# Fourteen commands of a one-core attention-and-MLP schedule at other places

## The chip, the core and the metric

The kernel runs on one core of a Trainium2 chip. The core has five engines, each with a queue of its own that it works through in order: TensorE (PE, matrix products; its weight loads have a row of their own in the profile, PEld), VectorE (DVE), ScalarE (ACT), GpSimd (POOL) and SyncE (SP, which here only starts transfers). They meet through semaphores. Sixteen DMA engines move data between memory and the chip; transfers are started from SP and ACT (queue q1 and q10 in the profile) and from POOL (queue q0). The metric is device time in microseconds (us), the median of several runs.

## What is computed

Attention for 4 batches of 8 heads, 768 positions, 64 values a head, and behind it an MLP whose hidden layer is the largest of three products:

```
scores = scale * q @ k.T                      # per batch and head
mask   = causal                               # heads 0, 2, 6 (retrieval)
mask   = causal & (sink | last 64 positions)  # heads 1, 3, 4, 5, 7 (near)
a      = exp(scores - max); a = a / (sum(a) + 1e-9)
x      = a @ v                                # 3072 rows of 512
h      = max(x @ w1, x @ w2, x @ w3)          # 512 -> 768
out    = h @ w_out                            # 768 -> 512
```

Inputs and output are in fp32; the products run in fp16 with fp32 sums.

## The kernel before

The order of the work is written out by hand. `PROGRAM` (lines 84 to 150) is a list of 493 short commands; the last loop of `fast` takes them one by one and calls the function that the first word names. Every engine gets its instructions in the order in which the commands issue them, so moving one command moves its instructions on every engine and every queue that it uses. Nothing is re-sorted behind that. A trailing letter names the engine of a copy (`d` DVE, `a` ACT, `p` POOL, `r` DVE in the form of a reduction over one element); `s` on a load is SP's queue.

A batch is worked in two halves of 384 positions. Batch 0 has a path of its own, so that the first scores can begin before much has landed: heads go in four pairs (0,2), (1,3), (4,6), (5,7), called hp 0 to 3. Later batches take keys and queries in two "quads" of four heads. The commands that the change and the prediction speak of:

- `hl half hp n`: loads of keys and queries of batch 0 in fp32 (SP and ACT). `cast half hp kq`: their casts to fp16, tiles `kn` and `qn`. `turnp half hp`: PE transposes them, and copies (line 241) bring them to `KQ`.
- `kx0 half hp` and `kx b quad`: copies of keys for the near heads' neighbouring blocks into `kx` (lines 561, 566; 573, 578).
- `s0 half unit hp..`: a score unit of batch 0. PE writes a mask (line 596) and the products (line 611) into one of two `st` buffers; ACT takes the exponential into `pt` (line 632). `s b n` is a score unit of the later batches (lines 677, 694). `k0` and `k` multiply a mask into `pt` (line 380).
- `load_v 0 half`: values of batch 0, three rows of a partition apart, into `vs`. `vc half h0 n`: their casts into `vn` (line 500). `vt half blocks`: PE sorts the rows by products with a 0/1 matrix `every3` (line 508) into banks `vb`, and casts bring them to `va` (line 513). `vt 0 02 da` sorts blocks 0 and 2, the first drained by DVE, the second by ACT.
- `y b half heads what`: copies values for the near heads into `vx`; `s` copies the sinks' rows (line 529), `r` the last rows (line 527).
- `av b half hp`: attention times values (line 720), normalised on DVE (lines 725, 727) into `x`. `x b half hp` transposes `x` on PE and copies it to `xT` (lines 743, 746); with `D` a DMA does that.
- `f b half w n`: a hidden unit, four products of weight w's block n with `xT` (line 440). Weight 0 is copied to `acc` (line 448), weights 1 and 2 take a maximum with it on DVE (line 452). `o`: the output product (line 465).
- `load b quad`: keys and queries of a batch's quad, cast on the way, started by POOL (line 261). `turn b quad i part`: DVE transposes them into `KQ` (line 275). `w n`: a weight's load, started by POOL. `gs n`: a tiny transfer on SP that holds SP's queue until a weight has landed. `flags`: fifteen tiny POOL operations on the flags `is_retrieval`.

Score units take the `st` buffers in turn, and products for `tr`, `vb`, `oacc` and `yy` take four banks in turn, so a unit waits until the one that held its place has been drained.

```
    for line in PROGRAM:
        for item in line.split(", "):
            name, *args = item.split()
            do[name](*args)
```

Of the kernel before, what the change touches and what calls it, by code (L numbers as in the profile page):

```python
# [83 lines left out]
PROGRAM = (  # L84
    "idle 11, hl 0 2 2 sc, cast 0 1 pd, turnp 0 1 aa, cast 0 0 dd, cast 0 2 dp, load_v 0 0 0 4 s",
    "load_v 0 0 4 4 s, turnp 0 0 ad, cast 0 3 pa, cleark 0 p, cleark 1 d, kx0 0 1 p, s0 0 1 1",
    "s0 0 0 0, hl 1 0 2 ss, idle 1, turnp 0 3 da, turnp 0 2 da, clear 0 d, s0 0 1 0, kx0 0 3 p",
    "s0 0 0 3, vc 0 0 4 p, vc 0 4 4 p, s0 0 0 1, kx0 0 2 p, s0 0 0 2, hl 1 2 2 ss, cast 1 0 dd",
    "turnp 1 0 dd, load 1 0 0, cast 1 1 pp, w 0, load 1 0 1, cast 1 3 dp, vt 0 02 da, cast 1 2 aa",
    "vt 0 1 a, turnp 1 1 d, y 0 0 1:4:2 r p, s0 0 1 2, s0 0 1 3, y 0 0 4:5:1 r r, turnp 1 3 ad",  # L90
    "s0 1 3 0, y 0 0 5:8:2 s r, kx0 1 1 p, y 0 0 1:4:2 s p, s0 1 1 1, load_v 0 1 s, turnp 1 2 dd",
    "kx0 1 2 r, y 0 0 5:8:2 r r, av 0 0 1, s0 1 2 0, kx0 1 3 p, w 1, gs 1, y 0 0 4:5:1 s p",
    "s0 1 0 1, av 0 0 0, av 0 0 3, av 0 0 2, s0 1 0 2, x 0 0 1 d, x 0 0 0 d, load 1 1, s0 1 3 2",
    "vc 1 0 4 p, x 0 0 3 a, vc 1 4 4 p, s0 1 0 0, s0 1 0 3, x 0 0 2 d, vt 1 1 a, turn 1 0 0 0",
    "clear 1 p, k0 1 1 2 p, vt 1 02 ad, turn 1 0 0 1, turn 1 0 1 1, s0 1 1 0, k0 0 0 2 p",
    "k0 0 1 2 d, f 0 0 0 3 a, k0 1 0 2 p, f 0 0 0 1 a, s0 1 1 3, w 2, y 0 1 1:4:2 r p, s0 1 1 2",
    "y 0 1 4:5:1 r r, gs 0, gs 0, gs 0, gs 0, k0 0 3 2 d, f 0 0 0 5 a, kx 1 0 a, k0 2 1 0 p",
    "turn 1 0 1 0, k0 3 0 2 p, av 0 1 0, av 0 1 1, f 0 0 0 4 a, turn 1 1 0 0, turn 1 1 0 1",
    "f 0 0 0 2 a, f 0 0 0 0 a, x 0 1 0 a, f 0 0 1 0, load 2 0, f 0 0 1 5, x 0 1 1 a, turn 1 1 1 1",
    "s0 1 2 2, k0 2 0 1 p, turn 1 1 1 0, f 0 0 1 3, f 0 0 1 2, k0 2 0 0 p, y 0 1 5:8:2 r a",  # L100
    "f 0 0 1 1, k0 3 1 2 p, f 0 0 1 4, s 1 0, av 0 1 2, kx 1 1 p, k0 2 1 1 p, k0 2 3 1 p",
    "av 0 1 3, f 0 0 2 0, f 0 0 2 1, s 1 1, x 0 1 2 a, f 0 0 2 5, k 1 0 X 1 d, k 1 1 Y 0 p",
    "f 0 0 2 2, turn 2 0 0 0, f 0 0 2 4, turn 2 0 1 0, x 0 1 3 a, s 1 2, f 0 0 2 3, f 0 1 0 5 a",
    "f 0 1 0 3 a, k 1 1 X 1 p, turn 2 0 1 1, f 0 1 0 1 d, s 1 7, k 1 2 X 0 p, f 0 1 0 2 d, flags",
    "load_v 1 0 s, v 1 0 0 d, y 1 0 1:8:2 s a, v 1 0 1 a, gs 0, k 1 2 Y 0 d, y 1 0 4:5:1 s r",
    "k 1 0 Y 0 p, f 0 1 0 0 d, w 3, v 1 0 2 d, f 0 1 1 2, s 1 3, f 0 1 2 2, f 0 1 1 1",
    "load_v 1 1 s, k 1 3 Y 0 p, f 0 1 1 3, f 0 1 2 3, y 1 0 4:5:1 r a, y 1 0 1:8:2 r a, gs 0",
    "f 0 1 0 4 d, s 1 5, k 1 0 X 0 d, k 1 1 X 0 p, load_v 2 0 s, f 0 1 1 5, f 0 1 2 5",
    "y 1 1 1:8:2 r r, k 1 7 X 1 p, y 1 1 4:5:1 r r, f 0 1 1 4, k 1 5 X 1 p, av 1 0 0 D, s 1 6",
    "load 2 1, av 1 0 1 D, v 1 1 2 d, f 0 1 1 0, v 1 0 3 a, f 0 1 2 0, f 0 1 2 1, k 1 2 X 1 p",  # L110
    "av 1 0 2 D, av 1 0 3 D, s 1 4, k 1 4 X 1 p, k 1 4 Y 0 p, f 0 1 2 4, v 1 1 3 p, o 0 0 0 a",
    "o 0 0 1 a, k 1 3 X 1 p, o 0 1 1 a, k 1 7 Y 1 d, turn 2 1 0 1, turn 2 1 1 1, k 1 4 X 0 p",
    "v 1 1 1 p, turn 2 1 0 0, turn 2 0 0 1, v 1 1 0 p, load_v 3 0 s, v 2 0 0 a, o 0 0 2 a, guess",
    "turn 2 1 1 0, f 1 0 0 1 a, f 1 0 0 0 a, f 1 0 1 0, f 1 0 0 5 d, k 1 7 X 0 p, v 2 0 1 p",
    "f 1 0 0 4 d, s 2 0, k 1 3 X 0 p, f 1 0 2 0, k 1 7 Y 0 d, load 3 0, k 1 6 X 0 p, f 1 0 1 4",
    "k 1 5 Y 0 d, v 2 0 2 a, y 2 0 1:8:2 s a, kx 2 0 d, kx 2 1 a, f 1 0 2 4, f 1 0 1 1",
    "k 1 5 X 0 d, f 1 0 0 3 a, f 1 0 1 5, f 1 0 1 3, k 1 6 Y 0 p, av 1 1 3 D, av 1 1 1 D, s 2 1",
    "k 2 1 Y 0 p, av 1 1 0 D, y 2 0 1:8:2 r a, f 1 0 2 3, k 2 0 Y 0 p, gp 1 2, f 1 0 2 1",
    "y 2 0 4:5:1 s a, av 1 1 2 D, k 2 1 X 0 p, y 2 0 4:5:1 r a, v 3 0 0 p, s 2 4, f 1 0 2 5",
    "f 1 0 0 2 d, load 3 1, y 3 0 4:5:1 r d, v 2 0 3 a, f 1 0 1 2, f 1 0 2 2, s 2 2, k 2 2 X 0 d",  # L120
    "f 1 1 0 0 d, k 2 1 X 1 p, k 2 0 X 1 p, f 1 1 0 4 a, f 1 1 1 0, y 3 0 1:8:2 s a, k 2 2 X 1 d",
    "turn 3 0 0 0, y 3 0 1:8:2 r p, f 1 1 0 5 d, load_v 3 1 s, s 2 7, f 1 1 0 2 d, k 2 0 X 0 p",
    "f 1 1 0 1 a, o 0 1 0 d, f 1 1 1 1, av 2 0 0 D, k 2 4 Y 0 d, f 1 1 1 2, f 1 1 1 5",
    "load_v 2 1 s, k 2 4 X 1 d, k 2 7 Y 1 d, f 1 1 1 4, k 2 7 X 0 d, o 1 0 2 d, s 2 3",
    "k 2 3 X 1 p, turn 3 0 1 0, gs 0, k 2 2 Y 0 d, f 1 1 0 3 a, o 0 1 2 a, av 2 0 1 D, s 2 6",
    "y 2 1 1:8:2 r a, f 1 1 2 0, k 2 6 X 0 p, av 2 0 3 D, f 1 1 1 3, k 2 7 Y 0 d, s 2 5",
    "k 2 6 Y 0 d, av 2 0 2 D, f 1 1 2 4, f 1 1 2 3, f 1 1 2 5, turn 3 1 0 1, k 2 3 X 0 p",
    "y 3 0 4:5:1 s a, o 1 0 1 a, k 2 5 X 1 p, turn 3 0 1 1, turn 3 1 1 1, k 2 3 Y 0 p, v 3 1 0 d",
    "v 2 1 2 a, o 1 0 0 a, k 2 7 X 1 p, f 1 1 2 2, f 2 0 0 0 a, f 1 1 2 1, f 2 0 1 0, k 2 4 X 0 d",
    "f 2 0 2 0, f 2 0 0 1 a, turn 3 1 1 0, f 2 0 0 2 d, f 2 0 1 2, y 2 1 4:5:1 r p, v 3 0 3 p",  # L130
    "v 3 1 2 a, v 2 1 0 a, turn 3 1 0 0, f 2 0 0 4 a, f 2 0 1 4, v 3 1 1 p, turn 3 0 0 1",
    "v 2 1 1 p, kx 3 0 d, f 2 0 0 3 d, y 3 1 1:8:2 r d, k 2 5 Y 0 d, f 2 0 1 3, f 2 0 2 3",
    "o 1 1 0 a, s 3 1, k 3 1 X 0 p, f 2 0 1 1, av 2 1 2 D, k 2 5 X 0 d, f 2 0 2 1, av 2 1 1 D",
    "av 2 1 0 D, v 2 1 3 a, k 3 1 Y 0 d, s 3 0, o 1 1 2 a, kx 3 1 d, av 2 1 3 D, v 3 0 2 a",
    "v 3 0 1 d, k 3 0 X 1 d, f 2 0 2 4, v 3 1 3 p, f 2 0 0 5 a, y 3 1 4:5:1 r d, s 3 2",
    "k 3 2 Y 0 d, f 2 0 1 5, o 1 1 1 d, k 3 0 X 0 p, f 2 0 2 2, f 2 1 0 4 a, k 3 2 X 1 p, s 3 4",
    "f 2 1 1 4, f 2 1 0 3 a, f 2 1 2 4, k 3 4 Y 0 p, f 2 1 0 5 d, f 2 0 2 5, f 2 1 0 0 a",
    "f 2 1 1 0, k 3 0 Y 0 p, f 2 1 2 0, k 3 4 X 0 d, k 3 1 X 1 p, s 3 7, av 3 0 1 D, f 2 1 0 1 a",
    "av 3 0 2 D, f 2 1 1 3, f 2 1 2 3, k 3 2 X 0 p, av 3 0 3 D, k 3 7 X 0 d, av 3 0 0 D",
    "f 2 1 1 1, s 3 3, k 3 4 X 1 d, k 3 3 X 1 d, f 2 1 2 1, o 2 0 2 d, k 3 7 Y 1 p, f 2 1 0 2 d",  # L140
    "k 3 7 X 1 d, o 2 0 0 a, k 3 3 Y 0 p, s 3 6, k 3 6 Y 0 p, f 3 0 0 2 a, f 3 0 0 3 d, f 3 0 1 2",
    "k 3 6 X 0 p, f 3 0 1 3, f 3 0 0 1 a, f 3 0 1 1, s 3 5, f 2 1 1 5, f 2 1 2 5, f 3 0 0 4 d",
    "k 3 5 X 1 p, f 3 0 1 4, o 2 0 1 d, k 3 3 X 0 d, f 3 0 2 3, f 3 0 2 4, f 2 1 1 2, f 3 0 2 2",
    "k 3 5 Y 0 d, k 3 5 X 0 p, k 3 7 Y 0 p, av 3 1 3 D, f 2 1 2 2, gs 0, av 3 1 0 D, av 3 1 1 D",
    "av 3 1 2 D, f 3 0 2 1, f 3 0 0 5 d, check, f 3 0 0 0 a, o 2 1 1 d, o 2 1 2 a, verdict",
    "f 3 0 1 0, f 3 0 1 5, f 3 0 2 0, f 3 1 0 4 a, f 3 1 0 3 a, f 3 1 1 4, read, f 3 0 2 5",
    "f 3 1 0 1 d, f 3 1 0 5 d, f 3 1 0 0 a, f 3 1 0 2 d, f 3 1 1 2, f 3 1 1 3, f 3 1 1 5, gs 0",
    "o 2 1 0 a, f 3 1 1 0, f 3 1 2 0, o 3 0 1 d, o 3 0 2 d, o 3 0 0 a, f 3 1 2 2, f 3 1 2 3",
    "f 3 1 1 1, f 3 1 2 1, f 3 1 2 4, f 3 1 2 5, o 3 1 0 a, o 3 1 1 a, o 3 1 2 d, idle 1",
)  # L150


# [892 lines left out]
```

## Time and profile before

| | |
|---|---|
| Time of the runs, median (lowest to highest of 3) | 189.5 us (189.13 to 190.56) |
| Span of the profiled execution (no other time is shown for it) | 188.2 us |
| Share of the chain that ended last: PE, DMA | 78%, 13% |
| Bytes moved by the DMA engines | 26.30 MB |
| POOL's queue q0, share of 16 engines over the span | 23.4% |
| SP's queue q1, share of 16 engines over the span | 35.6% |

The profile shows one execution. A row of a timeline gives the start in us, the length in us, the engine, the line in the kernel, the operation, the tile written and the tile read, shape and type, and how many instructions were put together (x3); in square brackets stands the idle time of the engine just before it and what ended it. Rows that stand together may overlap by a few hundredths, since an engine starts one instruction while the last one drains.

### The profile page before, as it was taken

How to read it: one execution, taken by the hardware profiler on the slowest of the kernel's cores; microseconds unless marked ns; L12 is line 12 of the kernel's file. 1: busy time of each engine (PE TensorE's matmuls, PEld its weight loads, DVE VectorE, ACT ScalarE, POOL GpSimd, SP SyncE). 2: the span in 40 equal slices, each digit the busy share in tenths (PEclk: the TensorE clock that was granted, in tenths of full speed). 3: DMA queues.
4: the chain of work that ended last, by engine and by line, in shares of the span. 5: the costliest groups of instructions: out<-in, count | busy, mean ns of one | idle time of the engine just before them, and what ended most of it. 6: DMA issues, size and time to landing. Idle time of an engine off the chain costs nothing.

```text
span 188.2 us, 4755 instructions
## 1 busy us (share of the span) xinstructions
PE 178.9 (95%) x1863; PEld 105.4 (56%) x1863; DVE 144.1 (77%) x306; ACT 99.4 (53%) x161; POOL 83.0 (44%) x142
## 2 busy tenths in 40 slices
PE   7789898999999999999999999999999999999990
PEld 2355546566566456855555556655745574664550
DVE  3749997989899978888979899756874698574540
ACT  3399996368965648687096336764445301311110
POOL 7697899808884890199057002127213400000000
PEclk9999999999999999999999999999999999999999
DMA  5999999998799999439693301321231013301413
GB/s 172 325 329 275 213 212 208 212 229 188 163 130 158 144 280 185 127 74 236 156 262 80 112 0 56 66 80 56 41 87 74 0 62 69 129 0 56 167 56 120
DMA packets 43012, 26.30 MB, mean 140 GB/s; under 512 B 29802, under 2 KB 38506, under 8 KB 42986
## 3 DMA queue, kind: packets, MB, share of 16 engines
q1 hardware_dynamic: 37562, 17.24, 35.6%
q0 software_dynamic: 4192, 7.87, 23.4%
q10 hardware_dynamic: 1232, 0.85, 1.5%
q8 instruction: 15, 0.25, 0.6%
q14 instruction: 11, 0.09, 0.1%
HBM read 25.17 MB, written 6.29 MB: 167 GB/s over the span
## 4 chain that ended last, share of the span: by engine, by line
PE 78%; DMA 13%; DVE 2%; POOL 2%; ACT 2%; issue 1%; ACTq 0%; DVEq 0%; POOLq 0%
PE yy L440 44%; PE yy L465 15%; PE st L677 7%; PE oacc L720 7%; DMA kq<-in_k_dram 7%; DMA qs<-in_q_dram 5%; PE yst L440 3%; DVE KQ L275 2%; DMA ks<-in_k_dram 2%; PE yst L465 1%; DVE acc L452 1%; POOL vx L529 1%; ACT qn L220 0%; ACT pt L632 0%; POOL w1t L401 0%
## 5 line engine op out<-in xcount | busy, mean ns | idle before, releaser
L380 POOL TENSOR_TENSOR pt<-pt,kb 128x512 f16<-128x512 f16 (+5 forms) x53 | 48.3, 931 | 59.7 <-ACT pt L694 51.1
L694 ACT ACTIVATE pt<-st 128x1024 f16<-128x1024 f32 (+2 forms) x51 | 43.5, 908 | 25.1 <-PE st L677 24.7
L440 PE MATMUL yy<-xT,w2t 128*128 128x384 f16 x184 | 36.2, 326 | 0.0
L440 PE MATMUL yy<-xT,w0t 128*128 128x384 f16 x180 | 34.8, 326 | 0.0
L440 PE MATMUL yy<-xT,w1t 128*128 128x384 f16 x176 | 34.3, 326 | 0.0
L465 PE MATMUL yy<-woutt,hT 128*128 128x512 f16 (+1 forms) x138 | 31.4, 372 | 0.0
L452 DVE TENSOR_TENSOR hT<-yy,acc 128x384 f16<-128x384 f32 x46 | 25.2, 555 | 4.6 <-PE yy L440 2.9
L452 DVE TENSOR_TENSOR acc<-yy,acc 128x384 f16<-128x384 f32 x44 | 23.9, 554 | 6.2 <-PE yy L440 4.3
L275 DVE STREAM_TRANSPOSE KQ<-kq 128x384 f32<-128x384 f32 x24 | 25.5, 1131 | 1.3 <-DMA kq<-in_k_dram 1.1
L448 ACT CAST acc<-yy 128x384 f16<-128x384 f32 x27 | 12.9, 492 | 23.5 <-PE yy L440 21.4
L440 PEld LDWEIGHTS <-w0t 128*128 128x128 f16 x192 | 18.1, 98 | 12.8 <-issue 0.7
L440 PEld LDWEIGHTS <-w1t 128*128 128x128 f16 x192 | 17.8, 98 | 12.0 <-issue 0.6
L440 PEld LDWEIGHTS <-w2t 128*128 128x128 f16 x192 | 17.7, 98 | 11.8 <-issue 0.2
L465 PEld LDWEIGHTS <-hT 128*128 128x128 f16 x150 | 14.4, 98 | 15.3
L720 PEld LDWEIGHTS <-pt 128*128 128x128 f16 x472 | 17.2, 97 | 4.2 <-DVE pt L380 0.9
L720 PE MATMUL oacc<-va,pt 128*128 128x65 f16 x392 | 18.6, 193 | 0.8 <-DVE pt L380 0.8
L474 ACT COPY ot<-yy 128x512 f32<-128x512 f32 (+1 forms) x14 | 7.9, 565 | 21.5 <-PE yy L465 18.9
L727 DVE TENSOR_TENSOR x<-oacc,sums 128x384 f16<-128x384 f32 x32 | 17.8, 557 | 1.1
L632 ACT ACTIVATE pt<-st 128x1024 f16<-128x1024 f32 (+5 forms) x22 | 15.4, 769 | 0.4 <-PE st L611 0.2
L677 PE MATMUL st<-KQ 32*128 32x128 f16 (+2 forms) x342 | 15.2, 257 | 0.1
L380 DVE TENSOR_TENSOR pt<-pt,kb 128x256 f16<-128x256 f16 (+4 forms) x31 | 12.4, 405 | 2.1 <-ACT pt L694 2.1
L677 PEld LDWEIGHTS <-KQ 32*128 32x128 f16 x342 | 8.8, 92 | 6.8 <-issue 6.0
(117 smaller groups left out, 190.5 us busy)
## 6 DMA issues: line engine op xcount, KB each, us to landing
out_dram<-ot SPq DMA_DIRECT2D x23, 256.0 KB, 2.0
vs<-in_v_dram SPq DMA_DIRECT2D x18, 256.0 KB, 4.6
ks<-in_k_dram SPq DMA_DIRECT2D x8, 192.0 KB, 3.7
kq<-in_k_dram POOLq DMA_DIRECT2D x3, 384.0 KB, 8.1
kq<-in_q_dram POOLq DMA_DIRECT2D x3, 384.0 KB, 9.6
kq<-in_k_dram POOLq DMA_DIRECT2D x3, 288.0 KB, 5.7
kq<-in_q_dram POOLq DMA_DIRECT2D x3, 288.0 KB, 7.5
qs<-in_q_dram ACTq DMA_DIRECT2D x4, 192.0 KB, 4.9
```

What stands on the lines that cost most here:

```text
L275: nc.vector.transpose(out=dst.rearrange("c (p j) -> c j p", j=n)[:, j0:j1], in_=src.rearrange("c (j i) -> c j i", i=R),)
L380: engine.tensor_tensor(out=x, in0=x, in1=of_blocks(kb, pattern, rows), op=ALU.mult)
L440: nc.tensor.matmul(yy[:, 0:HALF], w_t[wi][:, ks, ni * P : (ni + 1) * P], xT[b, half, ks].rearrange("p a t -> p (a t)"), start=(ks == 0), s ...
L448: op(out=acc[b, half, ni], in_=yy[:, 0:HALF])
L452: nc.vector.tensor_tensor(out=acc[b, half, ni] if wi == 1 else hT[b, half, ni], in0=yy[:, 0:HALF], in1=acc[b, half, ni], op=ALU.max,)
L465: nc.tensor.matmul(yo[:, 0:n], hT[b, half, ns][:, tb * P : (tb + 1) * P], woutt[:, ns, c : c + n], start=(ns == 0), stop=(ns == NNB - 1),)
L474: op(out=ot[:, c : c + n], in_=yo[:, 0:n])
L632: nc.scalar.activation(out=pts[0, half, hp, u][:, r0:r1, c0:c1], in_=sts[hp][:, r0:r1, c0:c1], func=AF.Exp, scale=sc,)
L677: nc.tensor.matmul(sts["XY"[g // 2]][:, g % 2, c0 : c0 + n * P], KQ[rows, 0, ki * P : (ki + 1) * P] if kind == "p" else kx[b % 2][quad][ro ...
L694: nc.scalar.activation(out=pts[b, s, xy][:, r0:r1, c0:c1], in_=st[:, r0:r1, c0:c1], func=AF.Exp, scale=sc,)
L720: nc.tensor.matmul(o[:, i, r, 0 : D + 1], at[b, h, kind, ki, qi], vv[:, 0 : D + 1], start=(n == 0), stop=(n == len(todo) - 1), skip_group_ ...
L727: nc.vector.tensor_tensor(out=x, in0=o[:, :, :, 0:D], in1=rc.unsqueeze(3).to_broadcast([P, HB, 2, D]), op=ALU.mult,)
```

## The change

Fourteen commands stand elsewhere. In PROGRAM's order:

- `vt 0 02 da` and `y 0 0 1:4:2 s p` go ahead; before, the first stood behind the casts of half 1's pair 3, the second behind `kx0 1 1`. Now both stand right behind `kx0 0 2`.
- `s0 0 1 0` goes back, from ahead of `kx0 0 3` to behind those two. So half 0's sorting now stands ahead of the two score units `s0 0 1 0` and `s0 0 0 2`.
- `cast 1 3 dp` goes ahead of `load 1 0 1`.
- `load 1 1` goes back from behind `x 0 0 0` to behind `s0 1 0 0`, which puts it behind the casts `vc 1 0 4` and `vc 1 4 4` on POOL.
- `s0 1 1 2` goes ahead of `s0 1 1 3`.
- `f 0 0 0 4` goes ahead of `av 0 1 0`; `f 0 0 1 5` goes ahead of `turn 1 1 0 0`; `f 0 0 1 0`, `load 2 0` and `f 0 0 1 2` change places behind it.
- `x 0 1 2` goes behind `f 0 0 2 5`; `flags` goes from behind `f 0 1 0 2` to ahead of `f 0 1 2 0`; `av 1 0 2` goes behind `av 1 0 3` and `s 1 4`.

Four commands have another engine: `x 0 0 3` goes from ACT to DVE, and `y 3 0 4:5:1 r`, `y 3 1 1:8:2 r` and `y 3 1 4:5:1 r` go from DVE to ACT. No instruction is added or left out. The list is one line longer, so every line behind it has its number raised by one in the changed kernel (line 513 is 514 there).

Of the list, the two lines that hold most of it:

```diff
-    "s0 0 0 0, hl 1 0 2 ss, idle 1, turnp 0 3 da, turnp 0 2 da, clear 0 d, s0 0 1 0, kx0 0 3 p",
+    "vc 0 0 4 p, vc 0 4 4 p, s0 0 0 1, kx0 0 2 p, vt 0 02 da, y 0 0 1:4:2 s p, s0 0 1 0, s0 0 0 2",
...
-    "s0 1 0 1, av 0 0 0, av 0 0 3, av 0 0 2, s0 1 0 2, x 0 0 1 d, x 0 0 0 d, load 1 1, s0 1 3 2",
+    "s0 1 3 2, vc 1 0 4 p, x 0 0 3 d, vc 1 4 4 p, s0 1 0 0, load 1 1, s0 1 0 3, x 0 0 2 d",
```

POOL's queue near 12 us, from the last copy of half 0's far keys (`kx`) on, before:

```order
L566 COPY kx_156<-KQ 128x4x4
L261 DMA kq<-in_k_dram 128x1536
L220 CAST kn<-ks 128x384
L220 CAST qn<-qs 128x384
L401 DMA w0t<-in_moe_w_dram 128x4x768
L261 DMA kq<-in_q_dram 128x1536
L220 CAST qn<-qs 128x384
L527 COPY vx_153<-va_151 64x2x2x64
L561 COPY kx_155<-KQ 128x2x64
L529 COPY vx_153<-va_151 64x8x64
```

and in the changed kernel:

```order
L567 COPY kx_156<-KQ 128x4x4
L530 COPY vx_153<-va_151 64x8x64
L262 DMA kq<-in_k_dram 128x1536
L221 CAST kn<-ks 128x384
L221 CAST qn<-qs 128x384
L402 DMA w0t<-in_moe_w_dram 128x4x768
L221 CAST qn<-qs 128x384
L262 DMA kq<-in_q_dram 128x1536
L528 COPY vx_153<-va_151 64x2x2x64
L562 COPY kx_155<-KQ 128x2x64
```

The copy of the sorted values (from `va` to `vx`, 64x8x64) went from behind the casts and the loads to ahead of all of them, and one cast of `qn` stands ahead of the load of queries.

POOL's queue near 19 us, from the copy into `vx` for the last near head on, before:

```order
L529 COPY vx_153<-va_151 64x4x64
L261 DMA kq<-in_k_dram 32x1536
L261 DMA kq<-in_k_dram 96x1536
L261 DMA kq<-in_q_dram 32x1536
L261 DMA kq<-in_q_dram 96x1536
L500 CAST vn<-vs 128x768 x2
L387 MEMSET va_152 128x48
```

and in the changed kernel:

```order
L530 COPY vx_153<-va_151 64x4x64
L501 CAST vn<-vs 128x768 x2
L262 DMA kq<-in_k_dram 32x1536
L262 DMA kq<-in_k_dram 96x1536
L262 DMA kq<-in_q_dram 32x1536
L262 DMA kq<-in_q_dram 96x1536
L388 MEMSET va_152 128x48
```

The two casts of half 1's values (`vs` to `vn`) went ahead of the four transfers of batch 1's second quad.

DVE's queue near 11 us, from the clearing of `vx` on, before:

```order
L388 MEMSET vx_153 128x20
L220 CAST kn<-ks 128x384
L220 CAST qn<-qs 128x384
L241 COPY KQ<-tr 128x384 x2
L220 CAST kn<-ks 128x384
L513 CAST va_151<-vb 128x8x64
```

and in the changed kernel:

```order
L389 MEMSET vx_153 128x20
L514 CAST va_151<-vb 128x8x64
L221 CAST kn<-ks 128x384
L221 CAST qn<-qs 128x384
L242 COPY KQ<-tr 128x384 x2
L221 CAST kn<-ks 128x384
```

The drain of the sorted values (`vb` to `va`) went ahead of three casts and two copies.

121 rows, old and new, of the table PROGRAM are left out of this document.

## The prediction, before the changed kernel ran

> **What bounds the kernel now.** I read the page's head first, then the busy time of each engine in chosen stretches, then the chain of work that ended last, then the timelines of single engines between 9 and 38 us, and last the DMA queues in four stretches.
>
> ```profile
> span 188.2 us, 4755 instructions
> PE 178.9 (95%) x1863; PEld 105.4 (56%) x1863; DVE 144.1 (77%) x306; ACT 99.4 (53%) x161; POOL 83.0 (44%) x142
> ```
>
> TensorE (PE) is busy for 178.9 of 188.2 us. Where the other 9.3 us lie decides what any reordering can win:
>
> ```profile
> core 0: us, PE busy (x) PEld busy (x) DVE busy (x) ACT busy (x) POOL busy (x), PEclk, DMA share, GB/s
> 15.00:20.00 5.00, 4.66 (x77) 3.26 (x76) 4.89 (x10) 4.91 (x11) 3.80 (x10) 1.00 1.12 252
> ...
> 25.00:30.00 5.00, 4.18 (x62) 2.56 (x57) 4.64 (x8) 4.92 (x12) 4.61 (x6) 1.00 1.14 213
> ...
> 37.40:160.00 122.60, 122.53 (x1396) 74.20 (x1396) 102.00 (x220) 68.86 (x104) 51.40 (x80) 1.00 0.56 120
> ```
>
> From 37.4 to 160 us PE is idle for 122.60 - 122.53 = 0.07 us. So whatever moves PE at 37.4 us moves the end by the same amount, and edits that act between 37.4 and 160 us can win 0.07 us at most. In the two stretches ahead it is the other way: VectorE (DVE) and ScalarE (ACT) are busy for 9.5 and 9.8 of 10 us, PE for 8.8, and the DMA engines are full (a share over 1). The chain shows what hands over at 37.4 us (start, us, what):
>
> ```profile
> 19.96 12.38 DMA kq<-in_k_dram
> ...
> 32.46 0.78 DVE KQ L275
> ...
> 34.34 1.05 DVE acc L452 x2
> 35.39 1.99 DVE KQ L275 x2
> ...
> 37.43 0.61 PE st L677 x10
> ```
>
> The keys of batch 1's second quad (`load 1 1`) land at 32.34; DVE turns keys and queries in four transposes with two maxima of the hidden layer between them; at 37.43 the first score unit of batch 1 (`s 1 0`) has its last operand. PE itself stood ready at 37.03, after one earlier wait:
>
> ```profile
> 29.03 0.20 PE L720 MATMUL oacc<-va,pt 128*128 128x65 f16 x1 [0.82 <-DVE pt L380]
> ...
> 37.03 1.01 PE L677 MATMUL st<-KQ 32*128 32x384 f16 x18
> ```
>
> That is `av 0 1 0`, which waited 0.82 us for a mask on DVE.
>
> **Part 1: half 0's values sorted early.** `vt 0 02` and the copy `y 0 0 1:4:2 s` on GpSimd (POOL) now come before `s0 0 1 0`, `s0 0 0 2` and before POOL's first quad load.
>
> ```profile
> 11.87 0.59 PE L596 MATMUL st<-far,ident 128*128 128x512 f16 x2 [0.33 <-ACT pt L632]
> ...
> 12.78 0.49 PE L596 MATMUL st<-far,ident 128*128 128x512 f16 x3
> ...
> 13.97 1.58 PE L508 MATMUL vb<-vn,every 64*128 64x512 f16 x9
> ```
>
> ```profile
> 14.86 0.58 ACT L513 CAST va<-vb 128x512 f16<-128x512 f32 x1
> ```
>
> Without `s0 0 1 0` ahead, `s0 0 0 1` need not wait 0.33 us for ACT and starts at 11.5, behind `s0 0 0 3`; it costs the 12.78 - 11.87 = 0.91 us between two units; the sorting products start at 12.4, and their drain follows 14.86 - 13.97 = 0.89 us later, at 13.3. DVE's drain is a cast of 0.68 us that now heads its queue:
>
> ```profile
> 11.61 0.55 DVE L220 CAST kn<-ks 128x384 f16<-128x384 f32 x1 [0.77 <-DMA ks<-in_k_dram]
> 12.81 0.55 DVE L220 CAST qn<-qs 128x384 f16<-128x384 f32 x1 [0.64 <-DMA qs<-in_q_dram]
> 13.90 1.02 DVE L241 COPY KQ<-tr 128x384 f16<-128x384 f16 x2 [0.55 <-PE tr L238]
> ...
> 15.30 0.68 DVE L513 CAST va<-vb 128x512 f16<-128x512 f32 x1
> ...
> 22.86 1.01 DVE L746 COPY xT<-tr 128x384 f16<-128x384 f16 x3
> ...
> 25.34 0.69 DVE L513 CAST va<-vb 128x512 f16<-128x512 f32 x1 [0.42 <-PE vb L508]
> ...
> 28.45 0.52 DVE L380 TENSOR_TENSOR pt<-pt,kb 128x256 f16<-128x256 f16 x1
> ...
> 29.81 0.20 DVE L725 RECIPROCAL sums<-oacc 128x6 f32<-128x6 f32 x1
> ...
> 30.76 0.56 DVE L727 TENSOR_TENSOR x<-oacc,sums 128x384 f16<-128x384 f32 x1
> ```
>
> So the cast of `kn` that stood at 11.61 starts at 14.0, 2.4 us later. The idle 0.64 and 0.55 us and the 0.68 us gone from its old place absorb 1.87 us: +0.5 is the least. POOL is the other bound:
>
> ```profile
> 12.10 0.75 POOL L261 DMA_DIRECT2D kq<-in_k_dram  x1
> ...
> 15.83 0.51 POOL L220 CAST qn<-qs 128x384 f16<-128x384 f32 x1 [0.59 <-DMA qs<-in_q_dram]
> 16.88 0.40 POOL L527 COPY vx<-va 64x256 f16<-64x256 f16 x1 [0.54 <-ACT va L513]
> 17.34 0.29 POOL L561 COPY kx<-KQ 128x128 f16<-128x128 f16 x1
> 17.58 0.61 POOL L529 COPY vx<-va 64x512 f16<-64x512 f16 x1
> ...
> 19.45 1.03 POOL L261 DMA_DIRECT2D kq<-in_k_dram  x2
> 20.48 0.99 POOL L261 DMA_DIRECT2D kq<-in_q_dram  x2
> 22.06 1.59 POOL L500 CAST vn<-vs 128x768 f16<-128x768 f32 x2 [0.59 <-DMA vs<-in_v_dram]
> ...
> 28.43 0.39 POOL L527 COPY vx<-va 64x256 f16<-64x256 f16 x1
> ```
>
> The 0.61 us copy waits for DVE's drain (14.0) and ends at 14.6, so the first quad load is issued at 14.6 instead of 12.10. Queued behind it are the casts of `cast 1 1` and `cast 1 3`, on which PE's transposes wait, the copy of far keys at 17.34, on which a score unit waits, and the loads of the first two weights. They start 2.5 us late at first and, once the idle 0.59 and 0.54 us are used up, 1.4 us late at the far keys. Between +0.5 and +1.4 I take +1.0 us for DVE at 20 us, nearer the POOL row, because the transposes that DVE copies out stand on PE behind the unit that needs those far keys. ACT waits in the same places, and gets one copy off its queue where `x 0 0 3` goes to DVE; its wait ends ahead of the two others, so I charge nothing for it.
>
> On DVE that copy, behind the row of 22.86, costs 1.01 / 3 = 0.34 us, and the 0.42 us idle before 25.34 absorbs as much. So the mask that released `av 0 1 0` at 28.97 (the row of 28.45) comes about 0.9 us late, at 29.9.
>
> **Part 2: the second quad load behind the value casts.** `load 1 1` cost POOL 1.03 + 0.99 = 2.02 us that lay in a wait: the values of half 1 let POOL go on only at 22.06. Now POOL reaches that wait at about 20.2 (19.45, +1.4, less the 0.61 us copy gone ahead), casts from 22.06 to 23.65, and only then issues the loads. Everything behind is 2.0 us late, and the copy of 28.43 to 28.82, which `av 0 1 0` needs, ends at 30.8. The transfers are hidden: one quad's and two weights' bytes stand ahead of them in POOL's DMA queue, and the DMA engines are full from 25 to 30 us.
>
> **Part 3: hidden units moved.** `f 0 0 0 4` goes ahead of `av 0 1 0`, so 4 products fill part of the gap:
>
> ```profile
> 30.25 2.11 PE L440 MATMUL yy<-xT,w0t 128*128 128x384 f16 x12
> ```
>
> Three units in 2.11 us with their tail, 1.96 as they follow one another: 0.65 us each. `f 0 0 1 5` ahead of the transposes takes one maximum (1.05 / 2 = 0.53 us) out of DVE's last stretch.
>
> **The sum.** PE resumes `av 0 1 0` at 30.87 instead of 29.03. PE's own work to `s 1 0` was 37.03 - 29.03 = 8.0 us, now 8.0 - 0.65: ready at 38.2. On DVE: products of `av 0 1 0` out at 31.65 (29.81 - 29.03 = 0.78 us after the resume), four normalising steps 1.5 us (29.81 to 31.32), one maximum, two transposes 2.08, one maximum, two transposes 2.05: 38.3. Before, it was 37.4. So `s 1 0` is complete 0.9 us later, and with no idle time on PE behind it, the span is 189.1. If half 1's values land early enough that POOL is not late, PE resumes at 29.95 and the same steps end at 37.7: +0.3.
>
> Priced at nothing: the three `y 3` copies that go from DVE to ACT, `flags` later on POOL, the swap of `av 1 0 2` and `av 1 0 3`, `x 0 1 2` later, the swapped `s0 1 1` units. All but the last lie behind 37.4 us, where PE waited for nobody. If that cover were gone, the copies would cost their length on ACT, at most the 0.61 us of the copy of 17.58 each (it is the largest shape), 1.8 together; I take 0, since ACT is busy for 69 of 122.6 us there. POOL's later masks are 2 us late too, and POOL is busy for 51 of those 122.6 us: I take 0 and leave up to 0.5 for it in the upper end.
>
> The profiled execution has only its span, 188.2. The runs' median is 189.5 (189.13 to 190.56), 1.3 above it; I keep that distance. 189.5 + 0.9 = **190.4 us**, which is no change in the measure's terms: about 1% (1.9 us) is what a measurement of this kernel can tell from none.
>
> **Rivals.** First, slower: the queue of POOL's loads starts late. The queue rows (packets, MB, share) are for 12.8 to 16.3 us, 16.3 to 17 us, and 17 to 22 us:
>
> ```profile
> q1 hardware_dynamic: 1534, 1.14, 109.8%
> ...
> q0 software_dynamic: 32, 0.10, 70.7%
> ...
> q1 hardware_dynamic: 29, 0.02, 1.8%
> ```
>
> POOL's queue is q0. Issued at 12.10, it moved nothing before 16.3, when q1 had all but drained. If q0 waited for q1, an issue at 14.6 changes nothing. If it needed 4.2 us from issue to first packet, it starts at 18.8, everything in it lands 2.5 us later, the keys at 34.8, and DVE ends 2.08 + 0.53 + 2.05 us after that, at 39.5: +2.1, 191.6 us. It decides once q0 starts after about 17.6, since DVE reaches the keys only at 33.7 in the sum above, 1.3 us after they land. For the first: both rows change hands within 0.7 us. For the second: the 29 late q1 packets ran beside q0, so the queues do not exclude each other.
>
> The Trainium skill (DMA: Bandwidth & Descriptors, section on SWDGE, HWDGE and iDMA) says each DMA engine goes round its queues in turn. By that rule q0 would have shared the engines from its first descriptor on, so its start would follow its issue, and the sum would be this rival's. The trace agrees after 17 us and shows no sharing before 16.3.
>
> Second, a little faster: the drain does not hold up DVE and POOL. The keys still land at 32.34, so the least is two transposes, one maximum and two transposes from 32.46: `s 1 0` complete 0.53 us earlier, 189.0 us. For it: the 0.82 us gap is filled, and DVE idled 1.96 us between 10.8 and 13.9. Against it: a drain at 13.3 lies behind both of those casts. It decides if the masks and copies for `av 0 1 0` are done by 29.0, for which half 1's values must land before about 20. They were issued in the row
>
> ```profile
> vs<-in_v_dram SPq DMA_DIRECT2D x1, 768.0 KB, 10.5
> ```
>
> at 11.53, so they landed at 22.0, and the 29 late packets are theirs; with q0 away a little longer they could be 2 us sooner. No rival wins 1.9 us, since the keys' landing allows 0.5.
>
> **How the numbers follow.** Forecast with both ends (+0.3 to +0.9, with small extra waits to +1.4): 0.66. Late q0: 0.18. A little faster: 0.13. Anything else: 0.03. The range takes in the second rival, the scatter below the median (0.4) and the first rival: 188.8 to 191.8. Faster by over 1%: 0.03; within 1%: 0.81, from the forecast and the second rival; slower by over 1%: 0.16, nearly all of it late q0.
>
> **What would show it.** In the changed profile: DVE's first cast of the sorted values ends near 14.0; POOL's first quad load is issued near 14.6; q0's first packets come at 16.3 to 17 (or near 18.8); half 1's values are cast at 22.06 and two quad loads follow at once; `av 0 1 0` resumes near 30.9 behind a POOL copy; `s 1 0` is complete near 38.3, and PE is full from there. It is wrong if `s 1 0` comes before 37.4, if the keys land after 33.7, or if PE shows new idle time behind 40 us.

## The result: 1.3 us slower, and the profile after

| | before | changed |
|---|---|---|
| Time, median (lowest to highest) | 189.82 us (189.13 to 190.62, 20 runs) | 191.12 us (189.99 to 191.80, 20 runs) |
| Ratio, 95% interval | | 1.0065 [1.0049, 1.0081] |
| Profiled execution, span | 188.2 us | 188.3 us, in a run of 190.38 us |

The two spans agree while the medians lie 1.3 us apart, and that has to be cleared up before the profiles are compared. In all thirteen profiled executions whose run time is known, and in the 97 runs of the kernel before that were made beside the experiments, the run takes 2.0 to 2.2 us more than its span. So the execution shown for the kernel before took about 190.3 us, 0.5 us above its median; the one of the changed kernel lies 0.7 us below its own. Executions differ from the first loads on, where the programs are still the same: POOL's first cast of values, behind such a load, starts at 9.91 us in the one profile and at 10.75 in the other, and between 9.77 and 11.26 in all that follow. So a profile tells where a wait stands; what it is worth is read from the medians.

First the timeline of DVE in the changed kernel, then POOL's (start, length in us, engine, line, operation; in brackets the idle time ahead and what ended it):

```profile
13.25 0.69 DVE L514 CAST va<-vb 128x512 f16<-128x512 f32 x1 [2.20 <-PE vb L509]
...
21.12 0.20 DVE L726 RECIPROCAL sums<-oacc 128x6 f32<-128x6 f32 x1
```

```profile
14.00 0.61 POOL L530 COPY vx<-va 64x512 f16<-64x512 f16 x1 [1.27 <-DVE va L514]
14.56 0.77 POOL L262 DMA_DIRECT2D kq<-in_k_dram  x1
16.24 0.78 POOL L402 DMA_DIRECT2D w0t<-in_moe_w_dram  x1
17.46 0.53 POOL L262 DMA_DIRECT2D kq<-in_q_dram  x1
...
18.97 0.75 POOL L402 DMA_DIRECT2D w1t<-in_moe_w_dram  x1
...
20.05 1.60 POOL L501 CAST vn<-vs 128x768 f16<-128x768 f32 x2
21.59 1.03 POOL L262 DMA_DIRECT2D kq<-in_k_dram  x2
```

The early sort does what it was forecast to do: DVE's drain ends at 13.94, POOL's first quad load is issued at 14.56, and DVE reaches its first normalising step at 21.12 instead of 20.08. But half 1's values are cast at 20.05 without a wait, not at 22.06: they had landed by 18.3 (issued at 11.90), since the transfer took 6.4 us instead of 10.5.

```profile
vs<-in_v_dram SPq DMA_DIRECT2D x1, 768.0 KB, 6.4
```

The timeline of PE:

```profile
18.84 0.23 PE L612 MATMUL st<-KQ,kx 64*128 64x128 f16 x2 [0.65 <-POOL kx L562]
...
30.87 0.82 PE L441 MATMUL yy<-xT,w1t 128*128 128x384 f16 x4
...
36.94 0.88 PE L678 MATMUL st<-KQ 32*128 32x384 f16 x18
...
60.73 0.20 PE L721 MATMUL oacc<-vx,pt 128*128 128x65 f16 x1 [0.58 <-POOL pt L381]
```

Both waits are new. At 18.84 a score unit of batch 0 stands until POOL has copied its far keys, which are late behind the sort; the wait at 60.73 lies where the forecast had PE full. `s 1 0` comes at 36.94, not at 38.3, and without a wait. The busy time of the engines in chosen stretches (columns as in the forecast) shows both:

```profile
15.00:20.00 5.00, 4.24 (x51) 2.44 (x53) 4.36 (x9) 4.38 (x10) 4.89 (x11) 1.00 1.08 235
25.00:30.00 5.00, 4.92 (x52) 2.70 (x52) 4.97 (x9) 5.00 (x11) 4.25 (x5) 1.00 1.14 210
30.00:37.40 7.40, 7.40 (x83) 4.62 (x83) 6.91 (x12) 4.01 (x10) 7.39 (x11) 1.00 1.12 211
37.40:160.00 122.60, 122.02 (x1396) 73.96 (x1385) 100.08 (x217) 70.18 (x107) 51.32 (x81) 1.00 0.56 121
```

PE lost 0.42 us between 15 and 20 us (4.66 before) and 0.51 behind 37.4 (122.53 before), and gained 0.74 between 25 and 30 (4.18 before). The wait at 60 us is that of `av 1 0 2` for a mask. Here is POOL ahead of that mask:

```profile
56.44 0.51 POOL L262 DMA_DIRECT2D kq<-in_q_dram  x1
56.93 0.09 POOL L758 MEMSET want<- 1x8 f32 x1
...
59.39 0.17 POOL L770 CAST flagged<-both 1x2 int32<-1x2 f32 x1
59.53 1.14 POOL L381 TENSOR_TENSOR pt<-pt,kb 128x512 f16<-128x512 f16 x1
```

The fifteen tiny operations of `flags` now fill 56.93 to 59.56, between the loads and the mask. Before, the same mask started at 57.19, at the end of the loads, and POOL was idle for 3.41 us behind it:

```profile
57.19 1.19 POOL L380 TENSOR_TENSOR pt<-pt,kb 128x512 f16<-128x512 f16 x1
61.80 1.82 POOL L380 TENSOR_TENSOR pt<-pt,kb 128x512 f16<-128x512 f16 x2 [3.41 <-ACT pt L694]
```

### The profile page after: what moved, and what is told of

It reads as the page before. It is cut to its first block, busy times and chain, and to the rows that moved or that the text cites. A ratio compares the mean times of both kernels' runs of the same rounds, so it can differ in the third digit from the quotient of the medians.

```text
span 188.3 us, 4757 instructions
## 1 busy us (share of the span) xinstructions
PE 178.8 (95%) x1863; PEld 105.4 (56%) x1863; DVE 142.3 (76%) x304; ACT 100.5 (53%) x163; POOL 82.6 (44%) x142
## 4 chain that ended last, share of the span: by engine, by line
PE 80%; POOL 7%; DMA 3%; DVE 3%; ACT 2%; issue 2%; SPq 1%; POOLq 0%; ACTq 0%
PE yy L441 45%; PE yy L466 15%; PE st L678 7%; PE oacc L721 7%; PE yst L441 3%; DMA ks<-in_k_dram 3%; ACT pt L633 2%; POOL kq L262 1%; PE yst L466 1%; DVE KQ L242 1%; POOL pt L381 1%; DVE x L728 1%; POOL vn L501 1%; SPq L207 1%; PE st L612 1%
## 5 line engine op out<-in xcount | busy, mean ns | idle before, releaser
L441 PEld LDWEIGHTS <-w1t 128*128 128x128 f16 x192 | 17.7, 98 | 11.8 <-issue 0.6
L721 PEld LDWEIGHTS <-pt 128*128 128x128 f16 x472 | 17.2, 97 | 4.0 <-POOL pt L381 0.9
L721 PE MATMUL oacc<-va,pt 128*128 128x65 f16 x392 | 18.6, 193 | 0.0
L678 PE MATMUL st<-KQ 32*128 32x128 f16 (+2 forms) x342 | 15.1, 257 | 0.0
L449 DVE CAST acc<-yy 128x384 f16<-128x384 f32 x18 | 10.0, 559 | 3.6 <-PE yy L441 3.2
```

The lines of the kernel that those rows point to most:

```text
L441: nc.tensor.matmul(yy[:, 0:HALF], w_t[wi][:, ks, ni * P : (ni + 1) * P], xT[b, half, ks].rearrange("p a t -> p (a t)"), start=(ks == 0), s ...
L449: op(out=acc[b, half, ni], in_=yy[:, 0:HALF])
L678: nc.tensor.matmul(sts["XY"[g // 2]][:, g % 2, c0 : c0 + n * P], KQ[rows, 0, ki * P : (ki + 1) * P] if kind == "p" else kx[b % 2][quad][ro ...
L721: nc.tensor.matmul(o[:, i, r, 0 : D + 1], at[b, h, kind, ki, qi], vv[:, 0 : D + 1], start=(n == 0), stop=(n == len(todo) - 1), skip_group_ ...
```

## The experiments

Twelve kernels in three groups; each group shares its runs of the kernel before. "Undone" kernels are the changed kernel with one part put back; "alone" kernels are the kernel before with one part of the change. The kernels of the experiments keep the line numbers of the kernel before. The diffs give the commands one to a line. All ratios are against the kernel before, whose medians in the three groups were 189.88, 189.84 and 189.5 us. Differences in us are worked out from the ratios, not from the medians printed beside them; one between an "undone" kernel and the changed kernel is uncertain by about 0.6 us.

| part of the change | undone: ratio, 95% interval | alone: ratio, 95% interval |
|---|---|---|
| place of `flags` | 1.0019 [0.9989, 1.0049] | 1.0076 [1.0053, 1.0100] |
| early sort | 1.0004 [0.9980, 1.0028] | 1.0054 [1.0032, 1.0075] |
| `load 1 1` behind the casts | 1.0057 [1.0030, 1.0083] | 1.0037 [1.0018, 1.0056] |
| hidden units | 1.0096 [1.0070, 1.0123] (weight 1's only) | 0.9975 [0.9948, 1.0003] |

**The place of `flags`.** Undone, and alone:

```diff
 f 0 1 0 2 d
+flags
 load_v 1 0 s
...
 v 1 0 3 a
-flags
 f 0 1 2 0
```

> The changed kernel with only `flags` back at its old place. Theory F (POOL's flag operations now stand ahead of a mask on which av 1 0 2 waits): the wait of 0.58 us on PE near 60 us is gone, the ratio to before falls from 1.0065 to about 1.003. Theory S (the early sorting and the later loads cost what the prediction said, in most executions, and the profiled one was a lucky one): the ratio stays at 1.006 and another wait on PE takes the place.

```diff
 f 0 1 0 2 d
-flags
 load_v 1 0 s
...
 v 1 0 3 a
+flags
 f 0 1 2 0
```

> The kernel before with only `flags` moved to its later place. Theory F: PE waits about 0.6 us for a POOL mask near 60 us, ratio 1.003. Theory S: the wait exists but is no more than 0.2 us, ratio 1.000 to 1.001.

Undone: 190.28 us, 0.46% below the changed kernel, 0.9 us, and no wait near 60 us. Alone: 191.57 us, +1.45 us, and PE's wait is longer than in the changed kernel. Its timeline:

```profile
59.77 0.20 PE L720 MATMUL oacc<-vx,pt 128*128 128x65 f16 x1 [1.59 <-POOL pt L380]
```

The wait of 1.59 us accounts for the cost of 1.45. In the five profiles of kernels that have `flags` at the new place and the swap of the `av 1 0` units, the wait is 0.57 to 0.59 us; the eight profiles with `flags` elsewhere show none there. In the changed kernel `av 1 0 2` stands behind `av 1 0 3` and `s 1 4`, which gives PE 1.01 us of other work while the mask is late (1.59 - 0.58). So the swap that I had priced at nothing pays back a part of the flags' cost: 1.01 us by the waits, 0.55 (1.45 - 0.9) by the medians. The swap was not tried by itself.

Whether they cost by being late, or only by standing ahead of that mask, was tried by moving them three commands on:

```diff
-flags
 f 0 1 2 0
 f 0 1 2 1
 k 1 2 X 1 p
+flags
 av 1 0 3 D
```

> The changed kernel with `flags` three commands further back, behind POOL's mask for batch 1's unit 2 (`k 1 2 X 1`), where POOL idled 3.41 us before the change. Theory, the flags cost only because they stand between that mask and the loads ahead of it: the 0.6 us wait of PE near 60 us is gone and the ratio falls to 1.001 to 1.004. Rival, their 2.6 us make the next masks late in turn: PE shows a wait of 0.5 us or more between 60 and 65 us and the ratio stays at 1.005 to 1.008.

189.92 us, 1.0015 [0.9994, 1.0036]: the cost is gone, and between 37.4 and 160 us PE is busy for 122.43 of 122.60 us. The same work behind the mask costs nothing, since POOL idles there.

**The early sort.** Undone, and alone:

```diff
 clear 0 d
+s0 0 1 0
 kx0 0 3 p
...
 kx0 0 2 p
-vt 0 02 da
-y 0 0 1:4:2 s p
-s0 0 1 0
 s0 0 0 2
...
+load 1 0 1
 cast 1 3 dp
-load 1 0 1
+vt 0 02 da
 cast 1 2 aa
...
 kx0 1 1 p
+y 0 0 1:4:2 s p
 s0 1 1 1
```

> The changed kernel with the sorting of half 0's values, its copy, s0 0 1 0 and the cast of pair 3 back at their old places. Theory S: DVE is 1.0 us and POOL up to 2.5 us earlier, so s 1 0 is complete 0.3 to 0.9 us earlier: ratio 1.000 to 1.004. Theory F: av 0 1 0 and s 1 0 do not move by more than 0.2 us and the ratio stays near 1.006.

The second kernel makes the opposite edit in the kernel before.

> The kernel before with the early sort alone. Theory, the sort costs by itself what undoing it gave back: +1.0 to +1.2 us, ratio 1.005 to 1.007, and the first score unit of batch 1 (`s 1 0`) comes about 1 us later, counted from the first value cast on POOL. Rival, half of that cost arose only because `f 0 0 1 5` now stands where weight 1 has not landed yet: +0.3 to +0.6 us, ratio 1.001 to 1.003.

190.04 us undone (-1.16 us), 190.73 us alone (+1.03 us): the sort costs about 1.1 us with and without the rest of the change. In the second one's profile `s 1 0` comes 26.6 us behind POOL's first cast of values, 0.65 later than in that of the kernel with `flags` alone moved; I had expected about 1 us. The rival, by which half of it came from the early `f 0 0 1 5`, falls as far as the kernel without that unit goes.

Which queue carries the cost? This kernel is the changed one with only POOL's 0.61 us copy at its old place:

```diff
 vt 0 02 da
-y 0 0 1:4:2 s p
 s0 0 1 0
...
 kx0 1 1 p
+y 0 0 1:4:2 s p
 s0 1 1 1
```

> The changed kernel with only the 0.61 us copy on POOL (the sinks' rows of half 0) back at its old place; the sorting products and their casts stay early. Theory, the sort's cost goes through POOL's loads, which wait behind that copy: the first quad load is issued near 12.1 instead of 14.6 and the time falls by 0.6 to 1.2 us, ratio 1.000 to 1.003. Rival, the cost goes through DVE, where the early cast heads the queue: no change to the changed kernel, ratio 1.005 to 1.008.

190.11 us, 1.0027 [1.0008, 1.0046]: 0.7 of the sort's 1.1 us are gone, though DVE's early drain stays. Its timelines of POOL and of DVE:

```profile
10.52 1.60 POOL L500 CAST vn<-vs 128x768 f16<-128x768 f32 x2
12.44 0.77 POOL L261 DMA_DIRECT2D kq<-in_k_dram  x1
```

```profile
20.20 0.20 DVE L725 RECIPROCAL sums<-oacc 128x6 f32<-128x6 f32 x1
```

Counted from POOL's first cast of values, DVE gets to its first normalising step after 9.68 us (20.20 - 10.52); it is 10.33 to 10.37 us in the six profiles with the early sort and its copy, and 9.40 to 9.63 in six without the sort (10.17 in that of before). So 0.7 of the 0.9 us by which DVE is late come through POOL, where the copy waits for DVE's drain in front of casts and loads. On PE the same queue shows as the wait for the far keys: 0.64 to 0.65 us in the six profiles with the early sort and its copy, 0.41 in this one, and none in the seven without the sort:

```profile
17.83 0.23 PE L611 MATMUL st<-KQ,kx 64*128 64x128 f16 x2 [0.41 <-POOL kx L561]
```

**The second quad load.** Undone, and alone:

```diff
 x 0 0 0 d
+load 1 1
 s0 1 3 2
...
 s0 1 0 0
-load 1 1
 s0 1 0 3
```

> The changed kernel with only `load 1 1` back ahead of the value casts. Theory S: POOL's masks are no longer pushed behind 2.0 us of load issues in executions where half 1's values land late, so 0.3 to 0.9 us are won on the median, ratio 1.002 to 1.005. Theory F: no change, 1.006, since in the profiled execution the values landed before POOL reached them and POOL was not late.

The second kernel makes the opposite edit in the kernel before.

> The kernel before with `load 1 1` alone moved back behind the two casts of half 1's values. My forecast's Part 2: POOL stands 2.0 us later at the masks for `av 0 1 0`, so +0.9 us, ratio 1.003 to 1.006. Theory now: the values land when POOL's queue lets them, near 20 us, POOL casts them at once and little is late: 0 to +0.3 us, ratio 0.998 to 1.0015.

190.81 us undone (-0.15 us, not told from none), 190.30 us alone (+0.7 us). The two differ, and POOL's rows show one reason. Alone in the kernel before, POOL comes to the casts before the values have landed and waits, here for 0.77 us; the load that used to fill this time now stands behind the casts:

```profile
10.47 1.60 POOL L500 CAST vn<-vs 128x768 f16<-128x768 f32 x2
...
20.11 1.59 POOL L500 CAST vn<-vs 128x768 f16<-128x768 f32 x2 [0.77 <-DMA vs<-in_v_dram]
...
28.50 0.39 POOL L527 COPY vx<-va 64x256 f16<-64x256 f16 x1
```

The copy that `av 0 1 0` needs starts 18.0 us behind POOL's first cast of values (28.50 - 10.47). It is 18.2 and 18.6 us in the two other kernels without the early sort and with the load moved, and 17.2 to 17.4 in three with the load at its old place (18.5 in the profile of before). With the early sort and its copy POOL comes to the casts later and finds the values landed, and the copy starts 18.0 us behind the first cast in all six profiles, wherever the load stands. So the forecast's mechanism is there in the kernel before, at 0.7 to 1.4 us of POOL's time instead of 2.0, and missing in the changed kernel. How much of the 0.7 us it makes no profile settles. PE's wait ahead of `av 0 1 0` is for a mask on DVE, and less than the 0.82 us of the profile of before:

```profile
28.51 0.20 PE L720 MATMUL oacc<-va,pt 128*128 128x65 f16 x1 [0.46 <-DVE pt L380]
```

That execution ran in 189.66 us, 0.6 below the kernel's median, so the slower ones may well be those in which the values come at 22 us, as in the profile of before. No trace of this kernel shows one.

**The hidden units.** Alone in the kernel before:

```diff
+f 0 0 0 4 a
 av 0 1 0
 av 0 1 1
-f 0 0 0 4 a
+f 0 0 1 5
 turn 1 1 0 0
...
 x 0 1 0 a
-f 0 0 1 0
-load 2 0
-f 0 0 1 5
+f 0 0 1 2
 x 0 1 1 a
...
 f 0 0 1 3
-f 0 0 1 2
+f 0 0 1 0
+load 2 0
 k0 2 0 0 p
```

> The kernel before with the moves of the hidden units alone (`f 0 0 0 4`, `f 0 0 1 5`, `f 0 0 1 2`, `f 0 0 1 0` with its load). Theory: this is the part of the change that gains, 0.4 to 0.7 us, ratio 0.996 to 0.998; the wait ahead of `av 0 1 0` (0.82 us before) falls to 0.2 us or less. Rival, batch 1's keys set the end of the stretch whatever stands ahead: ratio 0.999 to 1.001.

189.17 us, 0.9975 [0.9948, 1.0003]: 0.5 us faster by the ratio, the interval just reaching no change. In its trace `av 0 1 0` does not wait at all.

The next is the changed kernel with the units of weight 1 in their old order (the diff above the other way round, without `f 0 0 0 4`):

> The changed kernel with the hidden units of weight 1 (`f 0 0 1 5`, `f 0 0 1 2`, `f 0 0 1 0` with its load) back in their old order; `f 0 0 0 4` stays early. Theory, with the early sort weight 1 lands too late for the early `f 0 0 1 5` (PE waited 0.7 and 0.8 us for it in two of the runs above, and 0 in the changed kernel's own profile), so the new order loses what it gains: ratio 1.004 to 1.007. Rival, the new order gains here as in the kernel before: ratio 1.008 to 1.010.

191.12 us, 1.0096 [1.0070, 1.0123]: my theory falls. With the early sort the new order gains 0.6 us, much as without it, though each of the two gains is hardly larger than its uncertainty. The timelines of DVE and PE show what the old order does there:

```profile
33.03 2.09 DVE L275 STREAM_TRANSPOSE KQ<-kq 128x384 f32<-128x384 f32 x2 [2.13 <-DMA kq<-in_k_dram]
```

```profile
35.56 2.11 PE L440 MATMUL yy<-xT,w1t 128*128 128x384 f16 x12 [1.51 <-DVE acc L452]
```

DVE stands 2.13 us in front of the second quad's keys, and PE's later hidden units then wait 1.51 us for their maxima. In the changed kernel `f 0 0 1 5` gives DVE a maximum in that time, ahead of the transposes:

```profile
32.24 0.56 DVE L453 TENSOR_TENSOR acc<-yy,acc 128x384 f16<-128x384 f32 x1 [0.42 <-issue]
32.71 2.07 DVE L276 STREAM_TRANSPOSE KQ<-kq 128x384 f32<-128x384 f32 x2
```

**Combinations.** The changed kernel without the early sort and with `flags` at its old place, and the same with `load 1 1` back as well (the diffs above together):

> The changed kernel with both the early sort and the place of `flags` undone. Theory, the two costs add up: undoing the flags took 0.9 us off the changed kernel and undoing the sort 1.2 us, so this one stands at about 189.2 us, ratio 0.995 to 0.998, faster than the kernel before; PE shows no wait for a mask at 60 us. Rival, the two undone parts overlap (only the later of two waits counted): no faster than the better of the two single undos, ratio 1.000 to 1.002.

> The changed kernel with the early sort, the place of `flags` and the place of `load 1 1` undone, so that the hidden units and the small moves stay. Theory, `load 1 1` is worth nothing: ratio 0.996 to 0.998, about 189.2 us, as with `load 1 1` moved (0.997) and as with the hidden units alone (0.9975). Rival, my forecast's Part 2 holds: 0.9 us less again, ratio 0.991 to 0.994.

189.05 us both, 0.9969 [0.9942, 0.9996] and 0.9973 [0.9947, 1.0000]. So the costs of sort and flags add up within the intervals, and the place of `load 1 1` makes no difference here, where `f 0 0 0 4` stands ahead of `av 0 1 0`; that this unit covers it was not tried. The second differs from the hidden units alone (0.9975) by the small moves: the three `y 3` copies, `x 0 0 3`, `x 0 1 2`, the swapped `s0 1 1` and `av 1 0` units. Together they are worth nothing where `flags` does not stand in their way. All three are about 0.5 us faster than the kernel before by their ratios (0.9969 to 0.9975), and not to be ranked among each other.

## Why the forecast was near, and where its steps failed

The forecast of 190.4 us (188.8 to 191.8), no change by the bound of 1%, holds the time: +1.3 us where it had +0.9. That it does is in part luck: two misses of about 0.9 us, one each way, nearly cancel (Part 2 and the flags below), and the base of 189.5 us from three runs was 0.3 low. By the signs that it gave itself the forecast was wrong twice, since `s 1 0` came before 37.4 us and PE had new idle time behind 40.

**Part 1, the early sort: right in mechanism and cost, its positions by luck.** The drain at 13.94 for 14.0 and the first quad load at 14.56 for 14.6 agree because POOL's first cast of values began 0.84 us later in this execution than in the one the forecast started from. Counted from that cast, the load is issued after 3.8 us in all six profiles with the early sort and its copy, after 2.2 in that of before and 1.9 in six others: 1.6 to 1.9 us later, where the forecast had 2.5. The step that was off is the start of the sorting products: the forecast put them at 12.4, behind PE's score units, but in all seven profiles with the early sort they start within 0.1 us of the end of POOL's two casts of values (here 12.40 and 12.35). DVE is later by 1.0 us by the two profiles, and by 0.9 counted from POOL's first cast against the six profiles without the sort, for a forecast of 1.0. The choice for the POOL row over the DVE row was right: undoing the copy alone gives back 0.7 of the 0.9 us. The sort's cost is 1.0 to 1.2 us.

**Part 2, the second load: the step failed.** It took the landing of half 1's values at 22.0 us as fixed. They come with the timing of the queues: they took 6.4 to 6.5 us in all six profiles with the early sort and its copy, 8.4 to 9.5 in the others, and 10.5 only in the profile of before, which was an upper execution of its kernel. I had allowed for an early landing, at +0.3, and forecast the other case. The +0.3 was a slip besides: the same steps from 29.95 instead of 30.87 us end at 37.4, not 37.7, which is no change. POOL did not stand still, `av 0 1 0` ran at 29.48 without a wait, and `s 1 0` came at 36.94, not 38.3. In the changed kernel the load's place costs 0.15 us; alone it costs 0.7, near the 0.9 forecast, and there POOL is late in the way forecast, by 0.7 to 1.4 us instead of 2.0.

**Part 3, the hidden units: right as far as the intervals tell.** Forecast were 0.65 us of filled gap on PE and 0.53 us off DVE's last stretch; they are worth 0.5 us alone, and weight 1's units 0.6 us in the changed kernel.

**The flags: the term that was missed.** Step "all but the last lie behind 37.4 us, where PE waited for nobody" took a full PE for cover. That PE had no idle time says only that each operand came in time, not by how much. The row that counts was the mask that `av 1 0 2` needs: it ended at 58.38 (57.19 + 1.19), and PE used it here, in the timeline of before:

```profile
59.20 0.19 PE L720 MATMUL oacc<-vx,pt 128*128 128x65 f16 x1
```

2.6 us of new work on POOL ahead of it could not fit into 0.8 us; the 1.8 us left over are near the 1.59 that PE waited with `flags` alone moved. I had weighed POOL's share of busy time in that stretch (51 of 122.6 us) instead of this one margin. It costs 0.9 us in the changed kernel by the medians, 0.58 by the wait in its profile.

**The rival "late q0": its mechanism fell, another took its place.** POOL's queue moved its first packets between 16 and 17 us as forecast, though issued 2.5 us later. Queue rows (packets, MB, share of 16 engines) of the changed kernel for 14 to 16 and 16 to 17 us:

```profile
q1 hardware_dynamic: 873, 0.66, 109.7%
...
q1 hardware_dynamic: 325, 0.24, 81.1%
q0 software_dynamic: 17, 0.05, 29.3%
```

But it was fed more slowly from there. The rows of q0 for 16 to 18, 18 to 20 and 20 to 22 us, before and then changed:

```profile
q0 software_dynamic: 101, 0.31, 78.2%
...
q0 software_dynamic: 244, 0.39, 107.7%
...
q0 software_dynamic: 274, 0.42, 115.2%
```

```profile
q0 software_dynamic: 68, 0.21, 62.1%
...
q0 software_dynamic: 187, 0.35, 103.7%
...
q0 software_dynamic: 247, 0.38, 111.2%
```

0.94 MB instead of 1.12: at 0.21 MB a us, 0.9 us of transfer. Weight 1 (issue plus its time to landing) lands at 30.8 to 32.4 us in the six profiles with the early sort and its copy, at 29.3 to 29.9 in seven others, 30.4 in that of before. Where `f 0 0 1 5` stands early, PE meets it: the timeline of the kernel with `flags` behind the mask has

```profile
31.44 0.82 PE L440 MATMUL yy<-xT,w1t 128*128 128x384 f16 x4 [1.02 <-DMA w1t<-in_moe_w_dram]
```

and with `flags` or `load 1 1` put back it is 0.73 and 0.82 us, while in the changed kernel's own profile the weight landed just as PE came to it (30.87). That profile lies 0.7 us below its kernel's median; that a wait for weight 1 makes the difference fits, and was not shown. Bytes alone do not explain the landing either: with `load 1 1` put back, q0 moved 1.10 MB up to 22 us and weight 1 still came at 30.8. This stays open.

The sum by undone parts: sort 1.16 + flags 0.87 + load 0.15 - units 0.59 = 1.6 us, measured 1.3; each term is uncertain by about 0.6 us.

One more slip was in the base. I kept a distance of 1.3 us between the span and the median, though the distance to the run's own time is 2.0 to 2.2. The profile of before thus showed an execution above its median, in which the values took 1.0 us longer to land than in any other, and its wait of 0.82 us ahead of `av 0 1 0` was taken for typical. The kernel with `flags` alone moved, which has the same commands up to 46 us, shows a quarter of it:

```profile
27.81 0.20 PE L720 MATMUL oacc<-va,pt 128*128 128x65 f16 x1 [0.21 <-DVE pt L380]
```

## What to carry to other kernels

A full engine tells nothing of how much room the work has that feeds it: before work is moved on another engine, take the one instruction behind the new place that the full engine waits for next, and compare the end of it with the time of its use. Moving the same work three commands, to behind that instruction, was worth 0.9 us here. And one small copy that waits at the head of a queue delays all the loads issued behind it; what it delays is counted in landings, not in its own 0.61 us.

## What the runs showed of the hardware

- A queue that is issued to early may move nothing while another is full. POOL's first quad load was issued at 11.8 to 15.1 us in the fourteen profiles, and in all of them q0 had no packet from 14 to 16 us, when q1 took 106 to 110% of the 16 engines, and its first between 16 and 17 us. The Trainium skill (DMA: Bandwidth & Descriptors, section SWDGE vs HWDGE vs iDMA) has the engines go round their queues in turn; these rows show no sharing before q1 ran down.
- The transfer of half 1's values, 768 KB at the end of SP's queue, took 6.4 to 6.5 us where q0 was fed late and 8.4 to 10.5 us where it was fed early, with the same transfers ahead of it on its own queue.
- The time outside the span was 2.0 to 2.2 us in all thirteen profiled executions for which both are known, and in the 97 further runs of the kernel before.
